# Attention and expert layer on one core: where a planning step and the fifth batch's row scatters stand in the GpSimd queue

## The chip, the cores and the metric

The kernel runs on one core of a Trainium2 chip. The metric is the device time in microseconds (us) of one execution; the time of a kernel is the median of its runs. Engine names are those of the profile: PE (TensorE matmul), PEld (its weight loads), DVE (VectorE), ACT (ScalarE), POOL (GpSimd) and SP (SyncE, which here only issues DMAs). Lines are written L743 for line 743 of the kernel.

## The reference

Attention with rotary embedding over 8 batches, 8 heads, 576 tokens and a head size of 64 gives 4608 rows of 512 numbers; each row then goes to the one of 8 experts that its gate picks.

```python
q_rot, k_rot = rotate(q), rotate(k)
scores = scale * q_rot @ k_rot.T;  attn = softmax(scores)
x = (attn @ v).transpose(0, 2, 1, 3).reshape(N, D)
logits = x @ w_gate + modality_bias[modality_id]
e_idx = argmax(logits, axis=1); gate_w = softmax(logits)[e_idx]
for e in range(E):
    mask = e_idx == e
    out[mask] = gate_w[mask, None] * (relu(x[mask] @ w1[e]) @ w2[e])
```

## The kernel before, in words

**Attention.** The work goes by 32 pairs of heads (numbered 0 to 31, four to a batch). For each pair SP loads the two rotation inputs (`load`, L352); POOL rotates them with four instructions on 128x1152 tiles: the cosine product (`T2`, L466), the sine product (`T1`, L468), their sum (`R`, L470) and, after ACT has written the rounded part `HI` (L457), the rest `LO` (L474). SP then copies both parts into the other half of the partitions (`swap`, L482, keys `SWH` and `SWL`, two DMAs each). PE forms the scores of the pair (`scores`, L497, units S0 to S8) from the parts and their swapped copies, DVE takes minima (L506), ACT exponentials (L515), PE transposes (L520), DVE and ACT copy those out of PSUM (L553, L457), PE multiplies with v (L578) and projects (L613), and DVE scales the output rows (L628 to L632).

**Routing.** After the fourth pair of a batch SP writes its rows to DRAM (`xout`, L638 and L640), and fifteen small steps (RK0 to RK14) on POOL, DVE, ACT and PE find each row's expert and place. Then each of five blocks of rows is loaded back (`back`, keys BK0 to BK4, L761 and L763; on SP for the first five batches, on POOL for the last three) into one of two buffers XL, used in turn, and scattered to its place by a DMA that POOL issues (`scatter`, keys SC0 to SC4, L743). A scatter waits for its block's load; a load waits until the scatter that last used its buffer has landed.

**Planning.** After five batches `plan0` (L785 on) finds which expert's weights the first five blocks of the expert layer need. It is a generator that is run in nine pieces with due times `pl`; a piece is a row of tiny POOL instructions, or one sum on DVE (`total`, L788). The fifth piece is the DVE sum `total(tk, t88)`, whose input the fourth piece writes on POOL (L810 to L817). The ninth is L852 to L863.

**Expert layer.** `m_plan` reads the plan into SP registers, `m_ix` (L1012) loads the row table of a block, which must have been scattered before, `m_rows` (L1035) loads the rows, `m_load1` (L1039) and `m_load2` (L1044) the weights, and PE multiplies (L1089 to L1427).

**The order of the work.** Everything up to the expert layer is a list of jobs with due times: a job of pair n stands at 14.438 n plus its key, from `KEYS` or, for some pairs, from `EDGE`; jobs of the expert layer stand at 14.438 x 31 plus their entry in `MOE`. The list is sorted, and the jobs are written out in that order. PE, ACT, DVE, POOL and SP each keep that order, so on each engine a waiting instruction holds up all that follow it. Due times only order the work; they are not times of the profile.

The jobs that the change concerns stand in this order now. POOL, batches 1 to 4 (n is the batch's last pair): T1 of pair n+10, LO of n+9, T2 of n+10, SC3, R of n+10, RK11, SC4, T1 of n+11, LO of n+10. For the fifth batch (n = 19) SC1 stands behind R of pair 27, SC3 behind LO of 28, SC2 behind T2 of 30, SC4 behind R of 31; its BK2 and BK4 stand in SP's queue among the work of pairs 27 and 28. DVE has the fifth plan piece behind a row minimum (MN8) of pair 25 and ahead of a copy (B_F1) and three more minima of that pair.

Of the kernel before, what the change touches and what calls it, by code (L numbers as in the profile page):

```python
# [25 lines left out]
NSB = 4  # L26
NA = 1 + NSA
NB_MAX = 20
# [27 lines left out]
}  # L56
SLOTS = {
    "S0": 1, "S1": 2, "S2": 3, "S3": 0, "S4": 2, "S5": 0, "S6": 2, "S7": 0, "S8": 1, "F0": 1, "F1": 3, "F2": 0, "F3": 3, "FA": 2,
# [72 lines left out]
        "LD1": -42.214,  # L131
    },
    19: {
        "BK0": 71.4, "BK1": 71.5, "BK3": 95.0, "BK2": 116.0, "BK4": 131.0,
        "SC3": 113.825, "SC2": 128.215, "SC4": 152.075,
    },
# [73 lines left out]
    setdma=(-399.9101, -371.7589, -36.5660, -104.6596),  # L210
    consts=(-3.3332, 30.1765),
    plan=(-34.727, -25.884, -5.857, 16.183),
    ix=(-13.525, 11.679, 11.775, 17.3),
    w1=(-33.501, -27.735, 15.231, -22.655),
    w2=(-4.011, 1.762, 12.647, -8.483),
    hi=(-22.046, 1.027, 19.87, 16.903),
# [8 lines left out]
    l1d=(22.8091, 22.8691, 24.6621, 24.6471),  # L225
    w1n=(20.502, 24.643, 23.254, 22.825),
    place=(14.247, 18.005),
    rows=(-13.5, 11.7, 20.6, 31.756, 31.757),
    pl=(-114.356, -102.856, -99.906, -88.406, -85.506, -73.956, -51.417, -48.907, -45.303),
    end=24.98,  # L230
)
PIN = "PE,Activation,DVE,Pool"
# [3 lines left out]
def tile_attention_moe(ctx: ExitStack, tc: tile.TileContext, qk, v, mod, wg, mb, w1, w2, rope, cf, ci, out):  # L236
# [19 lines left out]
    PLA = cst.tile([1, 3, NA], I32, name="PLA")  # L256
    PLB = cst.tile([1, 3, NSB + NB_MAX + 1], I32, name="PLB")
# [6 lines left out]
    def cview(name):  # L264
        o, n = CF_OFF[name]
        return CF[:, o:o + n]
# [121 lines left out]
    def setup():  # L388
        g = nc.gpsimd
        v_ = nc.vector  # L390
        v_.memset(EPS, 1e-9)
        v_.memset(ZERO, 0.0)
        for t in PD:
            v_.memset(t, 0.0)
        v_.memset(P4, 0.0)
        for t in Vs:
            v_.memset(t[64:128, 0, 4, :], 0.0)
            v_.memset(t[0:64, 1, 4, :], 0.0)
        v_.memset(G, 0.0)
        for t in HL + SW:  # L400
            for c in (0, TW - 64):
                v_.memset(t[:, :, c:c + 64].bitcast(F32), 0.0)
        for h in range(4):
            for s in range(2):
                g.tensor_copy(RW[s * 64:s * 64 + 64, h, :].rearrange("p (o c) -> p o c", o=2)[:, :, 0:32],
                              idf[s * 64:s * 64 + 64, s * 64:s * 64 + 64].rearrange("p (o c) -> p o c", o=2))
        g.memset(MI, 0)
        nonlocal TI
        TI = XG[0].rearrange("p t g f -> p (t g f)")[:, 0:XU]
        g.memset(TI, 0.0)  # L410
        for x in XL:
            g.memset(x[:, XU:XW], 0.0)
        g.memset(TI[:, DM:DM + 1].bitcast(I32), EMPTY)
        g.memset(ON, 1.0)
        g.memset(OH, 0.0)
        g.dma_start(out=CF, in_=cf)
        g.dma_start(out=VAL, in_=ci)
# [363 lines left out]
    def plan0():  # L781
        G_ = nc.gpsimd

        def t1(name, sh):
            return sm.tile([1] + sh, F32, name=name, tag=name, bufs=1)  # L785

        def total(o, i):
            nc.vector.tensor_reduce(o, i, op=ALU.add, axis=AX.X)  # L788

        most = NPL * S // SUP  # L790
        AB = AB9[:, 0:E]
        sl = cview("SL")[0:1]
        EBv = cview("EB")[0:1]
        tri = cview("TRI")[0:1].rearrange("p (a b) -> p a b", b=E)
        nf, nb, cum, ge, tk, a2, rem, hc = (t1(x, [E]) for x in ("nf", "nb", "cum", "ge", "tk", "a2", "rem", "hc"))
        G_.tensor_tensor(nf, RUN[0:1, NPL, :], EBv, op=ALU.subtract)
        th = t1("th", [most])
        G_.tensor_scalar(th, sl[:, 0:most], float(SUP), float(SUP), op0=ALU.mult, op1=ALU.add)
        full = t1("full", [E, most])
        sh = [1, E, most]  # L800
        G_.tensor_tensor(full, nf.unsqueeze(2).to_broadcast(sh), th.unsqueeze(1).to_broadcast(sh), op=ALU.subtract)
        G_.tensor_scalar(full, full, 0.0, None, op0=ALU.is_ge)
        yield
        total(nb, full)
        yield
        t88 = t1("t88", [E, E])
        G_.tensor_tensor(t88, tri, nb.unsqueeze(1).to_broadcast([1, E, E]), op=ALU.mult)
        total(cum, t88)
        yield
        G_.tensor_tensor(tk, cum, nb, op=ALU.subtract)  # L810
        G_.tensor_scalar(tk, tk, float(NSA), None, op0=ALU.min)
        G_.tensor_scalar(a2, cum, float(NSA), None, op0=ALU.min)
        G_.tensor_tensor(a2, a2, tk, op=ALU.subtract)
        G_.tensor_scalar(hc, a2, float(SUP), None, op0=ALU.mult)
        G_.tensor_tensor(rem, nf, hc, op=ALU.subtract)
        G_.tensor_scalar(rem, rem, float(BLK), None, op0=ALU.is_ge)
        G_.tensor_tensor(t88, tri, rem.unsqueeze(1).to_broadcast([1, E, E]), op=ALU.mult)  # L817
        yield
        total(tk, t88)
        yield  # L820
        G_.tensor_scalar(tk, tk, 1.0, None, op0=ALU.is_equal)
        G_.tensor_tensor(rem, rem, tk, op=ALU.mult)
        G_.tensor_scalar(AB, a2, 2.0, None, op0=ALU.mult)
        G_.tensor_tensor(AB, AB, rem, op=ALU.add)
        sh = [1, NSA + 1, E]
        cmp = t1("cmp", [NSA + 1, E])
        cs = cmp[:, 1:NSA + 1, :]
        shs = [1, NSA, E]
        G_.tensor_tensor(cs, cum.unsqueeze(1).to_broadcast(shs), sl[:, 0:NSA].unsqueeze(2).to_broadcast(shs), op=ALU.subtract)
        G_.tensor_scalar(cs, cs, 0.0, None, op0=ALU.is_le)  # L830
        G_.tensor_tensor(cmp[:, 0, :], rem, cview("W8")[0:1], op=ALU.mult)
        yield
        es = t1("pes", [NB_MAX + 1])[:, 0:NA]
        total(es, cmp)
        yield
        G_.tensor_scalar(es[:, 0:1], es[:, 0:1], -1.0, float(E), op0=ALU.mult, op1=ALU.add)
        G_.tensor_scalar(es, es, float(E - 1), None, op0=ALU.min)
        G_.tensor_copy(PLA[:, 0, 0:NA], es)
        ch = t1("ch", [NB_MAX])[:, 0:NSA]
        G_.tensor_tensor(ch, es[:, 1:NA], es[:, 0:NSA], op=ALU.subtract)  # L840
        G_.tensor_scalar(ch, ch, 0.0, None, op0=ALU.is_equal)
        G_.tensor_scalar(PLA[:, 2, 1:NA], ch, -1.0, 1.0, op0=ALU.mult, op1=ALU.add)
        G_.memset(PLA[:, 2, 0:1], 1)
        G_.tensor_scalar(ge, nb, -float(SUP), float(RS), op0=ALU.mult, op1=ALU.add)
        G_.tensor_tensor(cs, cs, ge.unsqueeze(1).to_broadcast(shs), op=ALU.mult)
        G_.tensor_tensor(hc, hc, EBv, op=ALU.add)
        G_.tensor_scalar(hc, hc, float(-E * RS), None, op0=ALU.add)
        G_.tensor_tensor(cmp[:, 0, :], hc, rem, op=ALU.mult)
        yield
        rb = t1("rb", [NB_MAX])[:, 0:NA]  # L850
        total(rb, cmp)
        G_.tensor_scalar(rb[:, 0:1], rb[:, 0:1], float(E * RS), None, op0=ALU.add)  # L852
        r2 = t1("r2", [NB_MAX])[:, 0:NSA]
        G_.tensor_scalar(r2, sl[:, 0:NSA], float(SUP), None, op0=ALU.mult)
        G_.tensor_tensor(rb[:, 1:NA], rb[:, 1:NA], r2, op=ALU.add)
        G_.tensor_scalar(PLA[:, 1, 0:NA], rb, float(E * RS), None, op0=ALU.min)
        e2 = t1("e2", [NSB + 1])
        G_.tensor_scalar(e2[:, 0:1], es[:, NA - 1:NA], 1.0, None, op0=ALU.add)
        G_.memset(PLB[:, 2, NSB + NB_MAX:NSB + NB_MAX + 1], 1)
        G_.memset(CP9[:, 0:1], 0.0)  # L860
        G_.memset(AB9[:, E:E + 1], 0.0)
        G_.tensor_scalar(EB9, sl[:, 0:E + 1], float(RS), None, op0=ALU.mult)
        G_.tensor_scalar(EBN, EBv, float(-E * RS), None, op0=ALU.add)  # L863
        planned_[0] = e2
        yield
# [614 lines left out]

    K = KEYS
    setup()
    pinned = {getattr(mybir.EngineType, x) for x in PIN.split(",")}
    order = ExitStack()
# [62 lines left out]
    def Z(nm, i, f, *a):  # L1547
        J(MOE[nm][i], "moe", z, f, *a)
# [10 lines left out]
    for i in range(2):  # L1559
# [3 lines left out]
        Z("te", i, m_tre, 0, i, 0)  # L1563
        Z("ted", i, m_tre, 0, i, 1)
    g = plan0()
    for i in range(9):
        Z("pl", i, next, g, None)
    end = MOE["end"]
    for i, (s, j) in enumerate(((0, 0), (1, 0), (1, 1), (2, 0), (2, 1))):
# [186 lines left out]
```

## Time and profile before

| what | us |
|---|---|
| median of three runs | 871.61 (868.73 to 873.98) |
| the profiled execution | 869.71 |
| its span, first to last instruction | 867.9 |
| PE busy | 833.6 |
| POOL busy | 460.3 |
| DVE busy | 709.0 |
| ACT busy | 611.8 |

The profile tells of one execution; times in its rows count from the first instruction. An engine's row says when an instruction began, how long it took, its line and what it writes and reads, and in brackets how long the engine stood idle before it and what ended that. SPq rows are the issuing of DMAs, not the transfers. Attention runs until about 460 us, the expert layer from there.

### The profile page before, as it was taken

How to read it: one execution, taken by the hardware profiler on the slowest of the kernel's cores; microseconds unless marked ns; L12 is line 12 of the kernel's file. 1: busy time of each engine (PE TensorE's matmuls, PEld its weight loads, DVE VectorE, ACT ScalarE, POOL GpSimd, SP SyncE). 2: the span in 40 equal slices, each digit the busy share in tenths (PEclk: the TensorE clock that was granted, in tenths of full speed). 3: DMA queues.
4: the chain of work that ended last, by engine and by line, in shares of the span. 5: the costliest groups of instructions: out<-in, count | busy, mean ns of one | idle time of the engine just before them, and what ended most of it. 6: DMA issues, size and time to landing. Idle time of an engine off the chain costs nothing.

```text
span 867.9 us, 24887 instructions
## 1 busy us (share of the span) xinstructions
PE 833.6 (96%) x9528; PEld 689.5 (79%) x9528; DVE 709.0 (82%) x1595; ACT 611.8 (70%) x1311; POOL 460.3 (53%) x372
## 2 busy tenths in 40 slices
PE   2999999999999999899999999999999999999996
PEld 2777777777777777676778989898989898989895
DVE  7788898888888888797898677989898989897562
ACT  2898889898898988796985536565656575656453
POOL 3999979989999899899513123023302020202021
PEclk9999999999999999999999999999999999999999
DMA  8776858969789696875867983357964512531340
GB/s 289 211 242 180 272 158 261 265 203 266 217 257 272 201 276 192 259 223 173 233 197 195 332 227 107 61 179 227 298 173 153 139 50 49 172 97 49 121 142 22
DMA packets 115499, 165.81 MB, mean 191 GB/s; under 512 B 30636, under 2 KB 76350, under 8 KB 115372
## 3 DMA queue, kind: packets, MB, share of 16 engines
q1 hardware_dynamic: 106204, 137.99, 55.4%
q0 software_dynamic: 7824, 24.53, 8.2%
q8 instruction: 77, 1.26, 0.6%
q10 hardware_dynamic: 1344, 1.62, 0.6%
q14 instruction: 50, 0.41, 0.2%
HBM read 118.14 MB, written 34.70 MB: 176 GB/s over the span
## 4 chain that ended last, share of the span: by engine, by line
PE 46%; DVE 2%; POOL 1%; ACT 1%; issue 1%; SPq 1%; DMA 1%; POOLq 0%; ACTq 0%; DVEq 0%
PE psY L1331 20%; PE psH L1207 14%; PE ps L578 2%; PE psY L1207 2%; PE ps L520 1%; PE ps L497 1%; PE psH L1089 1%; PE psY L1108 1%; DMA ST<-in_moe_w_dram 1%; PE ps L1089 1%; PE psH L1403 1%; PE psY L1427 1%; DVE W2L L454 1%; SPq L1035 0%; PE ps L613 0%
## 5 line engine op out<-in xcount | busy, mean ns | idle before, releaser
L506 DVE CUSTOM_DVE_ANT_1 sc<-ps,ZERO 128x576 f32<-128x576 f32 x288 | 206.9, 749 | 23.5 <-PE ps L497 10.1
L515 ACT ACTIVATE P<-sc,mn 128x576 f32<-128x576 f32 x256 | 195.6, 768 | 5.6 <-DVE mn L506 5.0
L497 PE MATMUL ps<-HL 64*128 64x288 f32 x960 | 170.2, 312 | 12.5 <-ACT HL L457 11.3
L497 PE MATMUL ps<-SW 64*128 64x288 f32 x960 | 169.9, 312 | 4.2 <-DVE ST L468 3.6
L497 PEld LDWEIGHTS ps<-HL 64*128 64x128 f32 x960 | 136.3, 190 | 17.7 <-ACT HL L457 11.3
L1119 POOL DMA_INDIRECT out_dram<-sc,ix x36 | 43.8, 1218 | 200.2 <-ACT sc L1118 192.9
L497 PEld LDWEIGHTS ps<-SW 64*128 64x128 f32 x960 | 136.2, 190 | 8.8 <-DVE ST L468 3.9
L578 PE MATMUL ps<-PH,AT 128*64 128x320 f32 (+1 forms) x1024 | 138.2, 412 | 3.8 <-DVE PH L553 3.6
L1207 PE MATMUL psH<-HL,W1H 128*128 128x256 f32 x600 | 126.4, 279 | 0.2 <-ACT HL L457 0.2
L1207 PE MATMUL psH<-HL,W1L 128*128 128x256 f32 x400 | 111.6, 279 | 0.0
L578 PEld LDWEIGHTS ps<-PH,AT 128*64 128x64 f32 x1024 | 67.9, 136 | 52.0 <-DVE PH L553 7.0
L553 DVE COPY PH<-ps 128x512 f32<-128x512 f32 (+1 forms) x160 | 98.4, 631 | 10.0 <-PE ps L520 8.2
L457 ACT ACTIVATE PH<-ps 128x512 f32<-128x512 f32 (+1 forms) x160 | 85.1, 550 | 28.3 <-PE ps L520 23.2
L520 PEld LDWEIGHTS ps<-idf,P 64*128 64x128 f32 x2304 | 86.1, 138 | 21.9 <-ACT P L515 11.5
L1331 PE MATMUL psY<-W2L,SW 128*128 128x512 f32 x256 | 101.3, 396 | 0.0
L520 PE MATMUL ps<-idf,P 64*128 64x64 f32 x2304 | 97.6, 225 | 3.6 <-ACT AT L457 1.4
L1331 PE MATMUL psY<-W2H,SW 128*128 128x512 f32 x256 | 100.9, 394 | 0.0
L1207 PEld LDWEIGHTS psH<-HL,W1H 128*128 128x128 f32 x600 | 98.8, 188 | 1.0 <-ACT HL L457 0.4
L474 POOL TENSOR_TENSOR HL<-ST,HL 128x1152 fp32r<-128x1152 f32 x31 | 82.3, 2656 | 24.9 <-ACT HL L457 24.9
L743 POOL DMA_INDIRECT XS<-XL,oi x40 | 46.1, 1153 | 80.5 <-DMA XL<-X 60.6
L470 POOL TENSOR_TENSOR ST<-ST 128x1152 f32<-128x1152 f32 x30 | 79.7, 2656 | 1.2
L1207 PEld LDWEIGHTS psH<-HL,W1L 128*128 128x128 f32 x400 | 75.2, 188 | 0.0
(286 smaller groups left out, 1835.5 us busy)
## 6 DMA issues: line engine op xcount, KB each, us to landing
ST<-in_moe_w_dram SPq DMA_DIRECT2D x88, 512.0 KB
ST<-in_qk_dram SPq DMA_DIRECT2D x62, 576.0 KB
SW<-HL SPq DMA_DIRECT2D x124, 216.0 KB
AT<-in_v_dram SPq DMA_DIRECT2D x32, 256.0 KB
X<-X SPq DMA_DIRECT2D x8, 1024.0 KB
XL<-X SPq DMA_DIRECT2D x20, 257.0 KB
XG<-XS SPq DMA_DIRECT2D x40, 128.0 KB
XS<-ZR SPq DMA_DIRECT2D x8, 514.0 KB
```

The source lines that it names most:

```text
L457: return nc.scalar.activation(o, i, AF.Copy, scale=scale)
L470: e.tensor_tensor(a, a, b, op=ALU.add)
L474: e.tensor_tensor(d["HL"][:, 1, o], a, d["HL"][:, 0, o].bitcast(F32), op=ALU.subtract)
L497: nc.tensor.matmul(ps[:, g, 0:288], t[:, wq, q0:q0 + P], t[:, wk, k0:k0 + 288], start=(m == 0), stop=(m == len(L) - 1))
L506: nc.vector.tensor_tensor_reduce(sc, d.pop(("S", u))[:, :, 0:288], ZERO.unsqueeze(2).to_broadcast([P, 2, 288]), 1.0, FMAX, ALU.add, ALU.mi ...
L515: nc.scalar.activation(p, sc.rearrange("p a b -> p (a b)"), AF.Exp, bias=mn, scale=-1.0, accum_out=d["sum"][:, u:u + 1])
L520: nc.tensor.transpose(ps[:, g, c:c + 64], src[r, k0:k0 + P], idf[r, r])
L553: alone(d["at", f], g, (nc.vector.tensor_copy if g else acopy)(o, i).ins, int(f[1] in "23B"))
L578: i = nc.tensor.matmul(pa[hh * 64:hh * 64 + 64, 0:c1 - c0], d["V"][:, hh, kt, :], r, start=(kt == 0), stop=(kt == 4))
L743: inst = nc.gpsimd.indirect_dma_start(out=XS, out_offset=bass.IndirectOffsetOnAxis(ap=oi[0:n, j:j + 1], axis=0), in_=xl[b, j][0:n], in_off ...
L1207: nc.tensor.matmul(ps[b][:, r * BLK:r * BLK + BLK], w[:, c, f0:f0 + P], x[:, c, :], start=(first and r == 0 and c == 0 and i == 0), stop=( ...
L1331: nc.tensor.matmul(po[t], hx[:, c, o:o + P], w[:, c, :], start=(k == 0 and c == 2 * q and i == 0), stop=(k == 3 and c == 2 * q + 1 and i = ...
```

## The change

It gives some jobs other due times, cuts the ninth plan piece in two, and moves one memset to the start.

```diff
 KEYS:
-    "SC2": 105.27, "SC3": 118.91, "SC4": 121.32,
+    "SC2": 105.27, "SC3": 109.7, "SC4": 124.1,
 EDGE[19]:
-        "BK0": 71.4, "BK1": 71.5, "BK3": 95.0, "BK2": 116.0, "BK4": 131.0,
-        "SC3": 113.825, "SC2": 128.215, "SC4": 152.075,
+        "BK0": 71.4, "BK1": 71.5, "BK3": 95.0, "BK2": 156.0, "BK4": 156.1, "SC1": 151.5,
+        "SC3": 152.5, "SC2": 159.0, "SC4": 160.0,
 MOE:
-    ix=(-13.525, 11.679, 11.775, 17.3),
+    ix=(-7.2, 11.679, 11.775, 17.3),
-    rows=(-13.5, 11.7, 20.6, 31.756, 31.757),
-    pl=(-114.356, -102.856, -99.906, -88.406, -85.506, -73.956, -51.417, -48.907, -45.303),
+    rows=(-7.0, 11.7, 20.6, 31.756, 31.757),
+    pl=(-114.356, -102.856, -99.906, -88.406, -82.0, -73.956, -51.417, -48.907, -45.303, -15.1),
 setup():
         g.memset(ON, 1.0)
+        g.memset(PLA[:, 2, 0:1], 1)
 plan0():
-        G_.memset(PLA[:, 2, 0:1], 1)
...
         G_.tensor_scalar(PLA[:, 1, 0:NA], rb, float(E * RS), None, op0=ALU.min)
+        G_.memset(PLB[:, 2, NSB + NB_MAX:NSB + NB_MAX + 1], 1)
+        yield
         e2 = t1("e2", [NSB + 1])
         G_.tensor_scalar(e2[:, 0:1], es[:, NA - 1:NA], 1.0, None, op0=ALU.add)
-        G_.memset(PLB[:, 2, NSB + NB_MAX:NSB + NB_MAX + 1], 1)
...
-    for i in range(9):
+    for i in range(10):
         Z("pl", i, next, g, None)
```

In the sorted list this gives the following orders. POOL, batches 1 to 4: T1 of pair n+10, SC3, LO of n+9, T2 and R of n+10, RK11, T1 of n+11, SC4, LO of n+10. Fifth batch on POOL: R of pair 31, SC1, SC3, RK0 of the seventh batch, the new tenth plan piece, SC2, LO of 31, SC4. On SP: ... `xout` of the seventh batch, the v load of pair 30, BK2, BK4, SWL and SWH of 31, the v load of 31, one weight load, then the first block's row table and rows (`ix`, `rows`), which before the change stood right behind SWH of 31. On DVE the fifth plan piece stands behind the copy B_F1 and three minima of pair 25.

## Rows read from the trace of the kernel before

**Rows 1.** The page: busy time of each engine, and the group of the row minima.

```profile
PE 833.6 (96%) x9528; PEld 689.5 (79%) x9528; DVE 709.0 (82%) x1595; ACT 611.8 (70%) x1311; POOL 460.3 (53%) x372
...
L506 DVE CUSTOM_DVE_ANT_1 sc<-ps,ZERO 128x576 f32<-128x576 f32 x288 | 206.9, 749 | 23.5 <-PE ps L497 10.1
```

**Rows 2.** Windows of 20 us: PE, PEld, DVE, ACT, POOL busy, granted clock, DMA share, GB/s.

```profile
340.00:360.00 20.00, 20.00 (x358) 15.52 (x353) 17.95 (x57) 17.45 (x45) 17.82 (x11) 1.00 0.69 203
360.00:380.00 20.00, 17.18 (x260) 12.94 (x260) 16.54 (x51) 16.65 (x43) 18.81 (x25) 1.00 0.88 253
380.00:400.00 20.00, 19.14 (x312) 14.76 (x310) 15.46 (x46) 16.64 (x43) 18.14 (x26) 1.00 0.54 166
400.00:420.00 20.00, 18.61 (x316) 13.97 (x312) 16.20 (x50) 15.97 (x45) 19.27 (x16) 1.00 0.65 186
420.00:440.00 20.00, 20.00 (x317) 15.35 (x319) 16.70 (x46) 18.47 (x48) 6.50 (x9) 1.00 0.86 252
```

**Rows 3.** Timeline of all engines, the plan's fourth and fifth piece.

```profile
362.78 0.31 POOL L817 TENSOR_TENSOR t<-CF,rem 1x64 f32<-1x64 f32 x1
...
363.12 0.21 DVE L788 TENSOR_REDUCE tk<-t 1x8 f32<-1x64 f32 x1 [2.75 <-POOL t L817]
...
363.26 0.67 DVE L553 COPY PH<-ps 128x512 f32<-128x512 f32 x1
...
363.99 2.38 PE L578 MATMUL ps<-PH,AT 128*64 128x320 f32 x16 [2.78 <-DVE PH L553]
```

**Rows 4.** Timeline of POOL, pairs 28 to 31.

```profile
386.80 1.05 POOL L743 DMA_INDIRECT XS<-XL,oi  x1 [0.16 <-issue]
...
404.37 1.09 POOL L743 DMA_INDIRECT XS<-XL,oi  x1 [0.18 <-issue]
...
408.25 2.64 POOL L470 TENSOR_TENSOR ST<-ST 128x1152 f32<-128x1152 f32 x1
...
425.70 2.67 POOL L474 TENSOR_TENSOR HL<-ST,HL 128x1152 fp32r<-128x1152 f32 x1 [2.95 <-ACT HL L457]
```

**Rows 5.** Timeline of POOL, the part of the ninth piece that moves, first and last.

```profile
400.65 0.21 POOL L858 TENSOR_SCALAR e<-pes 1x1 f32<-1x1 f32 x1
...
401.35 0.23 POOL L863 TENSOR_SCALAR EBN<-CF 1x8 f32<-1x8 f32 x1
```

**Rows 6.** Timeline of ACT, pair 30.

```profile
410.93 1.16 ACT L457 ACTIVATE HL<-ST 128x1152 fp32r<-128x1152 f32 x1 [3.31 <-POOL ST L470]
```

**Rows 7.** Timeline of PE, pair 30.

```profile
412.47 1.21 PE L520 MATMUL ps<-idf,P 64*128 64x64 f32 x32 [1.39 <-ACT AT L457]
```

**Rows 8.** Timeline of SP, the queue ahead of pair 31's swaps.

```profile
428.94 1.16 SPq L361 DMA_DIRECT2D AT<-in_v_dram  x2
430.19 2.47 SPq L482 DMA_DIRECT2D SW<-HL  x4
432.93 0.71 SPq L1012 DMA_DIRECT2D ix<-XS  x1
```

**Rows 9.** Timeline of PE, first scores of pair 31.

```profile
437.26 0.38 PE L497 MATMUL ps<-SW 64*128 64x288 f32 x1
```

**Rows 10.** Timeline of SP and of POOL, fifth batch: first block's load and its scatter.

```profile
345.49 0.81 SPq L761 DMA_DIRECT2D XL<-X  x2
...
349.02 1.02 POOL L743 DMA_INDIRECT XS<-XL,oi  x1 [2.18 <-DMA XL<-X]
```

**Rows 11.** Timeline of POOL, sixth batch: a block's load and its scatter.

```profile
468.51 0.59 POOL L761 DMA_DIRECT2D XL<-X  x1 [3.52 <-DMA XS<-XL,oi]
475.89 1.00 POOL L743 DMA_INDIRECT XS<-XL,oi  x1 [6.79 <-DMA XL<-X]
```

**Rows 12.** Timeline of SP and of PE, pair 29: its swaps and first scores.

```profile
399.52 2.79 SPq L482 DMA_DIRECT2D SW<-HL  x4
...
406.07 0.40 PE L497 MATMUL ps<-SW 64*128 64x288 f32 x1
```

**Rows 13.** Windows of 4 us near the start, columns as in rows 2.

```profile
24.00:28.00 4.00, 2.51 (x56) 2.28 (x58) 3.78 (x8) 3.67 (x9) 3.92 (x3) 0.97 1.05 270
28.00:32.00 4.00, 4.00 (x49) 4.00 (x48) 2.53 (x10) 3.73 (x9) 2.12 (x3) 0.60 0.38 109
```

**Rows 14.** Timelines of SP and PE: swaps and first scores around pair 12, then pair 23.

```profile
166.16 1.10 SPq L482 DMA_DIRECT2D SW<-HL  x2
...
175.68 0.29 PE L497 MATMUL ps<-SW 64*128 64x288 f32 x1
...
315.91 1.15 SPq L482 DMA_DIRECT2D SW<-HL  x2
...
325.02 0.40 PE L497 MATMUL ps<-SW 64*128 64x288 f32 x1 [0.42 <-DMA SW<-HL]
```

## The prediction

> **What bounds the kernel now.** I read the page first: PE is busy 833.6 us of the span of 867.9, the next engine 709.0 [rows 1]. So an edit is worth what it takes from, or adds to, the 34 us in which PE is not busy. The windows of 20 us then show where those lie in the stretch that the change touches: PE is busy all of 340 to 360 and of 420 to 440, and short by 2.82, 0.86 and 1.39 us in the three windows between, 5.07 in all [rows 2]. POOL is busy 17.8 to 19.3 us of each 20 from 340 to 420 and only 6.5 in the next one [rows 2]: through these pairs it works without a pause, so whatever stands in its queue delays the rotations behind it; after 420 it has time.
>
> Two gaps make up most of the loss. The first is a chain of three waits: DVE sits 2.75 us in front of the plan's fifth piece until POOL has written its input, the PSUM copy behind it on DVE starts late, and PE waits 2.78 us for that copy [rows 3]. The second is POOL's lateness: R of pair 30 ends at 410.89 [rows 4], ACT, which stood idle 3.31 us for it [rows 6], writes HI, and PE waits 1.39 us for the ACT copy queued behind HI [rows 7].
>
> **The fifth piece on DVE.** Its own 0.21 us stays; it goes behind the copy and three minima. DVE was free at 363.12 - 2.75 = 360.37; the copy takes 0.67 and each minimum 0.75 [rows 1, 3], so it comes to the sum at 363.3, and the input is there at 362.78 + 0.31 = 363.09 [rows 3]. The wait goes, and with it PE's 2.78. Nothing else on DVE asks for the sum, and POOL reads it pairs later. Bounds: 0 to -2.78; I take **-2.78**.
>
> **POOL's queue up to R of pair 30.** SC1, SC3 and SC2 of the fifth batch leave it, each about 1.05 to 1.09 us with 0.17 in front [rows 4], 3.7 together, and so does the end of the ninth plan piece, from 400.65 to 401.58 [rows 5], 0.93. With no idle time to swallow it, R of pair 30 ends 4.6 us earlier, at 406.3. PE, itself 2.78 earlier, would see no wait if R ended by 410.89 - 1.39 - 2.78 = 406.7. So the 1.39 goes too. One thing goes the other way: by pair 29 POOL has lost only two scatters, 2.5 us, while PE is 2.78 ahead, so some 0.3 comes back there. The pairs before that have less again: 27 and 28 are rotated 1.2 us earlier but needed 2.78 earlier, which takes 1.6 of their margin; I count that at nothing, with 1.6 as its bound. **-1.39 + 0.3**, between 0 and -1.39. BK2 and BK4 leave SP's queue there as well, two issues that no wait of PE hangs on.
>
> **The scatters' new place.** SC1 and SC3 come behind R of pair 31, where POOL idles 2.95 us [rows 4] and is 4.6 us ahead besides; they, and the 0.9 us of the tenth piece, cost nothing. SC2 is another matter. It waits for BK2, and SP issues BK2 only behind the v load of pair 30, whose issue ends at 430.10 [rows 8]. That load and the writing of the seventh batch ahead of it wait for buffers that PE and DVE free, so they keep PE's pace: against PE's work BK2 can't go earlier. Behind SC2 on POOL stands LO of pair 31, behind LO on SP its swaps, and behind the swaps on PE the first scores of pair 31, at 437.26 [rows 9]. In PE's time, BK2 is issued where the swaps are issued now, 430.19 [rows 8], 7.1 us ahead of those scores. The new chain:
> - the load, from issue to the start of its scatter: 349.02 - 345.49 = 3.5 us [rows 10] on SP, 475.89 - 468.51 = 7.4 us [rows 11] on POOL amid the weight loads. I take 3.5: same queue, same batch, same sizes;
> - the scatter: 1.1 [rows 4];
> - LO: 2.7 [rows 4];
> - both swaps, from first issue to the scores: their issue alone takes 2.5 [rows 8], and pair 29 had them 406.07 - 399.52 = 6.55 us after the first issue without a wait on PE [rows 12]. I take 4.3, near the middle.
>
> Together 11.6, less 7.1: PE waits **+4.5** us. From the low ends it is 2.3, from the high ends 10.7. BK4 lands beside this chain, and SC4 stands behind LO.
>
> **Row table and rows of the first block.** `ix`, issued at 432.93 now [rows 8], must wait for SC4 to land, so it and the rows go some 10 us later, past a weight load that they no longer hold up; the two weight loads and the plan read behind them go later in turn. PE's expert layer starts near 460, itself shifted by the wait above, which covers them: 0. If the cover were gone, each us late would be one of PE.
>
> **The fourth and fifth scatters of batches 1 to 4.** SC3 now runs ahead of LO of pair n+9, so that LO and its swaps come 1.2 us later. In pair 12 the swaps of LO are issued at 166.16 and first used at 175.68: 9.5 us, which become 8.3. In pair 23, behind the writing of a batch's rows, 325.02 - 315.91 = 9.1 us were not quite enough and PE waited 0.42 [rows 14]. So the cost is between 0 and 0.8 a batch, 3.2 in all; I take 0, since no batch is written just ahead of pair 12's swaps. SC4 passes T1 of pair n+11 only; what stands ahead of LO of n+10 stays the same sum. The two memsets are too short to matter.
>
> **Sum.** 869.71 - 2.78 - 1.39 + 0.3 + 4.5 = 870.3 against the profiled execution. That one lies 1.9 under the median of the three runs, so for a median I say **872.2**: the gain is real and is given back at pair 31.
>
> **The clock.** Near the start PE was busy only 2.51 of 4 us, and in the next window the granted clock fell to 0.60 of full speed, part of it at 1.2 GHz: 0.40 x 4 = 1.6 us lost [rows 13]. The wait of 2.78 us left the clock at 1.00 [rows 2]. A wait of 4.5 lies beyond that. The Trainium skill, page "TensorE: Matmul & The Clock Gate", section "HAM oscillation — how this bites in real kernels", holds that a PE left waiting for data long enough falls back to half clock and has to earn the full one again. By that rule the new wait would cost the 1.6 on top; one row here agrees with it and the other doesn't contradict it.
>
> **Rivals.**
> - *The gain stands.* If BK2's data and the swaps come so fast that the chain is within about a microsecond of 7.1, or POOL's order lets LO go first, PE keeps 3.9: 865.8, as a median 867.7. For it: pair 31's swaps have 7.1 us now and POOL idles. Against it: issue, scatter, LO and swap issue alone make 9.8 with the shortest load seen.
> - *The clock falls in the new wait*: 870.3 + 1.6 = 871.9, as a median 873.8.
> - *Slower: the load is slow.* BK2 queues behind 1 MB of written rows, v and weights. At the 7.4 of rows 11 PE waits 8.4 us at pair 31's first scores, and the clock falls: 870.3 + 3.9 + 1.6 = 875.8, as a median 877.7. It decides from a load of about 6 us on.
> - *The first four batches pay* 0.8 each at pairs 12, 16, 20 and 24: 873.5, as a median 875.4. For it: pair 23 shows how thin the margin can be. Against it: pair 12 itself shows no wait.
>
> **Chances.** Forecast 0.40, on its own 870 to 874.5 (a wait of 2.3 to 6.8 us at pair 31); the gain stands 0.25; the clock 0.15; slow load 0.12; first batches 0.08. What the runs can tell from no change is 0.5%, 4.4 us: faster is below 867.3, slower above 876.0. The gain that stands lies at that edge, so about half of it counts as faster, with little else: 0.14. Slower takes most of the slow load, and a third of the first batches and of a fallen clock that comes with a longer wait: 0.17. The rest is 0.69. The range runs from 866.8, nearly a microsecond under the gain that stands, to 877.3, which leaves out the half of the slow load that is slower still.
>
> **What the profile after would show.** If the steps hold: no DVE wait in front of L788 and no PE gap near 361; ACT's wait for R of pair 30 about 1 us and no PE gap near 411; the row of SC2 with an idle time ended by XL<-X, LO of pair 31 right behind it, and in front of PE's first L497 of pair 31 a wait of 2 to 7 us for SW<-HL. The forecast is wrong if that last wait is missing, if waits for SW<-HL appear in pairs 12 to 24 or 27 to 28, or if the first products of the expert layer wait for their rows.

## The result and the profile after

The changed kernel takes 875.27 us in the median of 22 runs (869.98 to 879.33); the kernel before, run beside it, 868.95 (22 runs). The ratio is 1.0070, 95% interval 1.0055 to 1.0085: it is slower by 0.7%, 6.3 us between the medians, just beyond the 0.5% that was set as the bound of "no change". The profiled execution took 874.81 us, its span is 873.0 at a mean granted clock of 0.994 (867.9 and 0.996 before). Behind line 415 the lines of the changed kernel are one further on: L506 is now L507, L743 is L744.

The windows that answer to [rows 2], with the next 20 us (PE, PEld, DVE, ACT, POOL busy, granted clock, DMA share, GB/s):

```profile
360.00:380.00 20.00, 19.72 (x300) 14.64 (x298) 17.21 (x53) 18.94 (x49) 19.13 (x25) 1.00 0.89 261
380.00:400.00 20.00, 19.80 (x316) 15.19 (x313) 17.08 (x53) 17.25 (x46) 18.09 (x23) 1.00 0.50 131
400.00:420.00 20.00, 20.00 (x338) 15.08 (x336) 17.12 (x50) 18.18 (x45) 17.83 (x14) 1.00 0.71 214
420.00:440.00 20.00, 12.72 (x171) 9.77 (x169) 9.99 (x28) 11.68 (x34) 5.84 (x8) 0.90 0.67 201
440.00:460.00 20.00, 20.00 (x369) 15.98 (x367) 17.48 (x49) 15.36 (x41) 2.53 (x7) 0.93 0.61 174
```

The 5.07 us that PE lacked between 360 and 420 have become 0.48. The price stands in the next window: 7.28 us, and a granted clock of 0.90 and 0.93 where it was 1.00. The gain is what the prediction said. In the timelines of DVE and ACT the plan's fifth piece, now behind the copies and three minima, waits for nothing (2.75 before, [rows 3]), and ACT's wait for R of pair 30 is 1.15 us instead of 3.31 [rows 6]:

```profile
361.43 0.20 DVE L789 TENSOR_REDUCE tk<-t 1x8 f32<-1x64 f32 x1
...
404.32 1.16 ACT L458 ACTIVATE HL<-ST 128x1152 fp32r<-128x1152 f32 x1 [1.15 <-POOL ST L471]
```

The chain of waits from 420 to 440 names every step of the loss (start, duration, what):

```profile
423.73 0.55 SPq L361
...
424.37 4.20 DMA XL<-X
...
429.34 1.04 POOL XS L744
430.39 0.03 issue
430.42 2.63 POOL HL L475
...
433.06 0.50 SPq L483
...
434.29 4.12 DMA SW<-HL
438.41 0.14 issue
438.55 1.50 PE ps L498 x8
```

SP issues the v load of pair 30 (L361) and then BK2 at 424.37; POOL, free since 418.68, starts SC2 when that load has landed, at 429.34; LO of pair 31 stands behind it, the swaps behind LO, and PE behind the swaps. The row of the first scores reads:

```profile
438.55 0.58 PE L498 MATMUL ps<-SW 64*128 64x288 f32 x1 [7.28 <-DMA SW<-HL]
```

Compared matmul by matmul, the 5.1 us by which the span grew come in five pieces. The row of pair 23's first scores stands at 323.56 instead of 325.02 [rows 14]: 1.46 us early. Of these, 0.84 arise between 24 and 33 us, where the kernel before ran in part at 1.2 GHz [rows 13] and this execution of the changed one did not:

```profile
28.00:32.00 4.00, 3.94 (x55) 3.23 (x55) 3.26 (x10) 3.93 (x12) 2.42 (x3) 1.00 0.42 120
```

That drop near 28 us comes and goes: seven of the fourteen profiles have it, a second one of the changed kernel (e5) among them. So this part of the lead is not the change's. Pair 31's scores could have begun at 438.55 - 7.28 = 431.27 instead of 437.26 [rows 9]: another 4.53 us early, the change's gain. The wait makes that 1.29 late. The next rows, of PE in the expert layer, stand at 498.81 against 495.61 before, 3.20 late: 1.9 us more, the clock, for all of it arises while the scores and transposes from 438.55 on run slowly (at 442.78 the changed kernel is already 3.23 late). The last, the rank products at 549.61 against 544.47, are 5.14 late: another 1.9, of which 1.47 is a longer wait (2.58 for 1.11).

```profile
498.81 0.39 PE L1208 MATMUL psH<-SW,W1H 128*128 128x256 f32 x1 [0.34 <-DVE SW L455]
...
549.61 0.18 PE L707 MATMUL psY<-OH,UT 128*128 128x48 bf16 x1 [2.58 <-DVE OH L695]
```

So -1.5 - 4.5 + 7.3 + 1.9 + 1.9 = 5.1. Most of the first is an accident of the two executions; which of the other four belong to the change was the question for the runs.

### The profile page after: what moved, and what is told of

It is laid out like the page before. It is cut to its first block, busy times and chain, and to the rows that moved or that the text cites. A ratio compares the mean times of both kernels' runs of the same rounds, so it can differ in the third digit from the quotient of the medians.

```text
span 873.0 us, 24884 instructions
## 1 busy us (share of the span) xinstructions
PE 834.8 (96%) x9528; PEld 690.2 (79%) x9528; DVE 708.7 (81%) x1595; ACT 612.0 (70%) x1311; POOL 460.6 (53%) x372
## 3 DMA queue, kind: packets, MB, share of 16 engines
q10 hardware_dynamic: 1344, 1.62, 0.6%
## 4 chain that ended last, share of the span: by engine, by line
PE 73%; DMA 9%; POOL 6%; ACT 4%; DVE 3%; issue 2%; SPq 2%; ACTq 0%; POOLq 0%; DVEq 0%
PE psY L1332 21%; PE psH L1208 14%; PE ps L579 12%; PE ps L498 12%; PE ps L521 7%; DMA SW<-HL 3%; PE psY L1208 2%; PE ps L614 2%; DMA ST<-in_moe_w_dram 2%; POOL HL L475 2%; POOL ST L471 2%; DMA XL<-X 1%; PE psH L1090 1%; PE psY L1109 1%; ACT P L516 1%
## 5 line engine op out<-in xcount | busy, mean ns | idle before, releaser
L507 DVE CUSTOM_DVE_ANT_1 sc<-ps,ZERO 128x576 f32<-128x576 f32 x288 | 206.9, 749 | 31.2 <-PE ps L498 17.9
L744 POOL DMA_INDIRECT XS<-XL,oi x40 | 46.4, 1161 | 91.3 <-DMA XL<-X 69.1
```

What stands on the lines that cost most here:

```text
L507: nc.vector.tensor_tensor_reduce(sc, d.pop(("S", u))[:, :, 0:288], ZERO.unsqueeze(2).to_broadcast([P, 2, 288]), 1.0, FMAX, ALU.add, ALU.mi ...
L744: inst = nc.gpsimd.indirect_dma_start(out=XS, out_offset=bass.IndirectOffsetOnAxis(ap=oi[0:n, j:j + 1], axis=0), in_=xl[b, j][0:n], in_off ...
```

## The experiments

Each run has 6 to 12 executions, beside 17 to 35 of the kernel before on the same chip. The medians of before differ from chip to chip (870.1 to 872.2 us), so kernels are compared by the ratio to their own before. The ratios and intervals are those on record; a ratio is not quite the quotient of the two medians (the widest gap is e2's, 0.9969 for 871.65 / 872.16 = 0.9994), so a difference of 0.2% between two ratios says little.

| run | edit | median us | ratio | interval |
|---|---|---|---|---|
| e1 | changed; SC2 behind LO of pair 31 | 871.06 | 0.9982 | 0.9957 to 1.0007 |
| e2 | changed; BK2 ahead of the seventh batch's rows | 871.65 | 0.9969 | 0.9943 to 0.9995 |
| e3, e11 | before; plan's pieces alone | 869.87, 868.95 | 0.9959, 0.9975 | 0.9936 to 0.9982, 0.9954 to 0.9995 |
| e4 | before; SC3, SC4 of batches 1 to 4 alone | 872.76 | 1.0001 | 0.9976 to 1.0026 |
| e5 | changed, again | 876.23 | 1.0056 | 1.0024 to 1.0088 |
| e6 | e1 with batches 1 to 4 as before | 869.49 | 0.9988 | 0.9960 to 1.0015 |
| e7 | changed; plan's pieces as before | 879.97 | 1.0095 | 1.0062 to 1.0128 |
| e8 | changed; BK2 ahead of the v load | 874.82 | 1.0039 | 1.0012 to 1.0066 |
| e9 | e6; SC1 ahead of R of pair 31 | 867.69 | 0.9951 | 0.9928 to 0.9975 |
| e10 | e6; SC1 and SC3 ahead of R of pair 31 | 869.49 | 0.9986 | 0.9965 to 1.0007 |
| e12 | changed; SC1 ahead of R; BK2, BK4 behind the swaps; SC2 behind LO | 870.50 | 1.0010 | 0.9989 to 1.0031 |

The first four tell the parts of the change apart.

**e1: SC2 behind LO.**

```
-        "SC3": 152.5, "SC2": 159.0, "SC4": 160.0,
+        "SC3": 152.5, "SC2": 159.25, "SC4": 160.0,
```

> The third scatter of the fifth batch goes behind LO of pair 31 instead of in front of it; all else is the changed kernel. Theory (the chain load, scatter, LO, swaps makes the wait at pair 31, and the wait brings the half clock): no wait over 1 us on PE in front of pair 31's first scores, no half clock near 436, the gain of about 4.6 us up to pair 31 stays: 868.95 - 4.6 = 864.4 us, between 863 and 866. Rival (the row table and the rows of the first block come too late by then): the wait at pair 31 goes too, but PE waits in the expert layer between 455 and 550 for 3 us or more, and the time is 867 to 869. Rival (the swaps themselves are slow behind the written rows of the seventh batch): a wait of 2 to 4 us for SW stays at pair 31, 867 to 870.

The wait at pair 31 is gone, and so is the half clock there; the ratio falls from 1.0070 (1.0056 in e5) to 0.9982, with intervals well apart. But 864.4 us was not reached, and neither rival shows: no wait for SW at pair 31, none over 1 us in the expert layer before the rank products. The timelines of DVE, PE and POOL show a cost that nobody had on the list:

```profile
421.19 0.76 DVE L507 CUSTOM_DVE_ANT_1 sc<-ps,ZERO 128x576 f32<-128x576 f32 x1 [1.58 <-PE ps L498]
...
422.01 2.37 PE L579 MATMUL ps<-PH,AT 128*64 128x320 f32 x16 [1.63 <-DVE mn L507]
...
418.31 1.10 POOL L744 DMA_INDIRECT XS<-XL,oi  x1 [0.16 <-issue]
419.71 0.99 POOL L744 DMA_INDIRECT XS<-XL,oi  x1 [0.30 <-issue]
```

DVE stands in front of the first row minimum of pair 30 till 421.19. The view names PE's scores, but PE's last score matmul of that stretch started at 420.08, and in the profile of the changed kernel this minimum started 0.85 us behind the first score matmul, here 2.71. SC1 and SC3, side by side, run on POOL in just that time. e6, e9 and e10 take this up.

**e2: the load earlier, SC2 left in front of LO.**

```
-        "BK0": 71.4, "BK1": 71.5, "BK3": 95.0, "BK2": 156.0, ...
+        "BK0": 71.4, "BK1": 71.5, "BK3": 95.0, "BK2": 151.6, ...
```

> The load BK2 goes ahead of the writing of the seventh batch in SP's queue, some 7 us earlier; SC2 stays in front of LO of pair 31. Theory (it is the late load, not the scatter's place on POOL): POOL has its input before it would want it, LO of pair 31 ends by 428, no wait over 1 us at pair 31, no half clock near 436, 864 to 866 us. Rival (the scatter in front of LO is the trouble whatever the load does): a wait of 3 us or more for SW stays at pair 31 and the time stays above 869. Either way BK2 has to wait on SP until the second scatter has read its buffer; if that holds SP for over 2 us, the v load of pair 30 comes later and a new wait for AT would show at pair 30.

Between the two. BK2 did not come 7 us earlier: the timelines of SP, POOL and PE show

```profile
420.63 0.36 SPq L1040 DMA_DIRECT2D ST<-in_moe_w_dram  x1
426.17 0.34 SPq L762 DMA_DIRECT2D XL<-X  x1
426.61 0.61 SPq L639 DMA_DIRECT2D X<-X  x1
...
429.53 1.04 POOL L744 DMA_INDIRECT XS<-XL,oi  x1 [6.55 <-DMA XL<-X]
...
438.93 0.37 PE L498 MATMUL ps<-SW 64*128 64x288 f32 x1 [2.15 <-DMA SW<-HL]
```

SP stands from 421.0 to 426.2 until SC1, which left POOL at 420.44, has read the buffer, 5.7 us. That is the second half of the trap: with two buffers a load can't go earlier than its scatter's landing. The wait at pair 31 is 2.15 us, with a clock of 0.85 from 440 to 450. The wait for AT at pair 30 that was thought of did not come. And the load itself was quick: ahead of the seventh batch's rows, not behind them, it took 429.53 - 426.17 = 3.36 us to the start of its scatter.

**e3 and e11: the plan's pieces alone.** The changed kernel with the fifth batch, the row table, the rows and batches 1 to 4 put back.

> Only the plan's pieces are moved and split; the fifth batch's loads and scatters, the fourth and fifth scatters of batches 1 to 4 and the first block's row table and rows stay where they were before. Theory (two gaps with two causes): the gap of 2.78 us near 361 goes, but POOL is only 0.93 us ahead, so PE, 2.78 us early, waits for R of pair 30 near 411 for 1.39 + 2.78 - 0.93 = 3.2 us; net 2.78 - 1.85 = 0.9 us faster than before, about 868.0 us (867 to 869). Rival (POOL's work follows PE's pace, so both gaps go with the plan piece alone): 868.95 - 4.2 = 864.8 us and no gap over 0.5 us near 411.

> The kernel with the plan's pieces alone moved and split, once more, as the yardstick for the two runs beside it. Theory (two gaps with two causes): no wait near 361, waits of 2 to 3.5 us in all for R or HI of pairs 28 to 30 between 370 and 415, no stall of DVE over 0.5 us in front of pair 30's first row minima (one scatter runs there, not two); ratio 0.996, within 0.998 and 0.9935. Rival (its ratio of 0.9959 owed much to clock that by chance did not fall): 0.998 to 1.000.

The gap at 361 is gone and others take its place, as the first theory said, but spread. In e3 PE waits

```profile
372.95 0.53 PE L521 MATMUL ps<-idf,AT 64*128 64x64 f32 x10 [0.62 <-DVE mn L507]
...
374.51 1.34 PE L521 MATMUL ps<-idf,P 64*128 64x64 f32 x32 [0.91 <-DVE mn L507]
...
389.37 0.26 PE L521 MATMUL ps<-idf,P 64*128 64x64 f32 x1 [0.45 <-issue]
...
399.13 0.71 PE L521 MATMUL ps<-idf,P 64*128 64x64 f32 x16 [0.72 <-ACT P L516]
...
412.70 1.46 PE L521 MATMUL ps<-idf,P 64*128 64x64 f32 x40 [0.66 <-ACT AT L458]
```

3.36 us in all, 3.50 in e11, against 2.14 in that stretch before (0.28, 0.47 and 1.39). Compared matmul by matmul with before, e3's PE gains 2.85 us near 361 and has 1.2 of them left at 413; e11's gains 2.86 and has 1.0 left. That is close to the 0.9 of the first theory. The times are further under before than that: 3.6 and 2.2 us by the ratio, 2.3 and 2.1 by the medians. The clock makes part of it: its mean over e3's runs was 0.9966 against 0.9946 for before, which is 0.0020 x 870 = 1.7 us.

**e4: batches 1 to 4 alone.**

```
-    "SC2": 105.27, "SC3": 118.91, "SC4": 121.32,
+    "SC2": 105.27, "SC3": 109.7, "SC4": 124.1,
```

> Only the fourth and fifth scatters of batches 1 to 4 are moved, on the kernel before. Theory: nothing waits for them, 869.0 us, within 1 us of before, and the gaps of PE up to pair 27 are those of before. Rival (each batch pays where LO is 1.2 us later): new waits for SW<-HL of 0.4 to 0.8 us in pairs 12, 16, 20 and 24, 870.5 to 872 us.

The ratio is 1.0001, and PE's waits over 0.15 us between 150 and 355 us are 0.24, 0.45 and 0.82 against 0.47, 0.40, 0.42 and 0.33 before, 1.51 in all for 1.62: no cost, as forecast. The kind of wait is another, though. All three of e4's are for SW (at pairs 11, 15 and 23); of before's only the 0.42 at pair 23 is, and the others are for copies of DVE. Over that stretch the waits for SW add up to 0.42 to 2.30 us in the eight profiles with the new places and to 0 to 1.11 in the six with the old, those of all kinds to 0.60 to 3.12 and 1.33 to 2.22. They stand at pairs 11, 15, 19 and 23 for the most part, and none at pairs 12, 16, 20 and 24, where the rival has them. The run tells something else. Its wait near 361 is that of before (3.02 us to 2.78), yet the window from 360 to 370 has a granted clock of 0.83 (e4 first, then the kernel before):

```profile
360.00:370.00 10.00, 6.98 (x69) 4.08 (x66) 4.71 (x14) 5.02 (x14) 9.22 (x13) 0.83 0.94 273
```

```profile
360.00:370.00 10.00, 7.22 (x118) 5.32 (x116) 6.65 (x19) 7.13 (x18) 9.22 (x14) 1.00 0.95 283
```

**e5, e7, e8: what sets the wait.** e5 is the changed kernel again. e7 takes back the plan's pieces, their times and the cut in two:

```
-    pl=(-114.356, -102.856, -99.906, -88.406, -82.0, -73.956, -51.417, -48.907, -45.303, -15.1),
+    pl=(-114.356, -102.856, -99.906, -88.406, -85.506, -73.956, -51.417, -48.907, -45.303),
```

e8 puts BK2 in front of pair 30's v load ("BK2": 152.1 for 156.0).

> The changed kernel itself once more, beside the next three on one chip, for what recurs in its profile. Theory (a chain of fixed steps makes the wait at pair 31): the wait in front of pair 31's first scores is there again, 6.5 to 8 us long, half clock follows it, and the time is 0.7% over before. Rival (the 7.28 us were one slow load): the wait is 4 to 5.5 us in this profile and the ratio falls to 1.003. The wait for OH near 547, 2.58 us in the first profile of this kernel and 1.11 before, is not tied to the change in either; if it recurs at 2.5 it is.

> The fifth batch's loads and scatters, the first block's row table and rows, and the places in batches 1 to 4 as changed, but the plan's pieces in their places of before. Theory (the chain at pair 31 keeps PE's pace, so what the plan's fifth piece saves is not swallowed by the wait): PE waits 2.8 us near 361 as before, not near 411, and 6.5 to 8 us at pair 31 with half clock behind; the time is 2 to 3 us over that of the changed kernel. Rival (the chain keeps time of its own, and PE only runs ahead into the wait): the wait at pair 31 is shorter by 2.8 us, about 4.5, and the time is that of the changed kernel within 0.5 us.

> The changed kernel with the load BK2 in front of the v load of pair 30 instead of behind it in SP's queue; SC2 stays in front of LO of pair 31. Theory (each us that BK2 is issued earlier is one less at pair 31): BK2 is issued some 2.5 us earlier against PE's work, the wait at pair 31 is 4.7 us (4 to 5.5), half clock follows for 3.4 or 6.8 us, and the time is 2.5 us or a little more under that of the changed kernel. Rival (the load waits for the second scatter to have read its buffer, which took 5.7 us in the run with the load still further ahead): BK2 is issued no earlier than 5.5 us behind that scatter, 421.8 us if it is issued where it was, so the two agree on the load; but where the scatter lands later still, SP stands, and the wait is 5.5 to 7 us.

The starts of the steps, from the timelines of SP, POOL and PE (us); the last column is from BK2's issue to the scores:

| | BK2 | SC2 | LO | swaps | scores | PE's wait | chain |
|---|---|---|---|---|---|---|---|
| changed | 424.37 | 429.34 | 430.42 | 433.06 | 438.55 | 7.28 | 14.18 |
| e5 | 425.69 | 430.28 | 431.35 | 434.03 | 439.61 | 5.50 | 13.92 |
| e7 | 433.61 | 438.50 | 439.51 | 442.16 | 447.67 | 7.71 | 14.06 |
| e8 | 424.27 | 429.94 | 431.01 | 433.70 | 439.28 | 3.99 | 15.01 |

The chain is 13.9 to 15.0 us in each: fixed steps, not one slow load. e5's wait of 5.50 missed the 6.5 to 8 that were expected and lies at the edge of what the rival gave; its chain of 13.92 and its ratio of 1.0056 speak against the rival. In e7, where PE waits for the plan's piece again (2.13 us), the wait is not shorter but 7.71: BK2 keeps PE's pace, so what PE gains ahead of it is not swallowed. Its time is 0.39% over e5's, 3.4 us, with intervals that overlap a little. In e8 BK2 is issued 435.28 - 424.27 = 11.0 us ahead of where the scores would begin, against 6.9 in the changed kernel, and the wait is 3.99, at the low end of the 4 to 5.5 expected; the ratio is lower than e5's by 0.17%, 1.5 us, with intervals that overlap. e5's wait is shorter because its BK2 has 434.11 - 425.69 = 8.4 us of head start for 6.9. Where the 1.5 come from was not tried; DVE's stall, seen in e1, held PE up 1.23 us near 419, and if SP's queue did not share that, it is most of them.

**e6, e9, e10: the stall.** In the seven profiles with SC1 and SC3 side by side behind R of pair 31 (changed, e1, e2, e5, e6, e7, e8), DVE stood 0.93 to 1.72 us in the first row minima of pair 30 in six, and PE 0.98 to 1.63 behind it in five; in the three without the pair (before, e3, e4), never. The seventh is the first profile of the changed kernel, where SC1 and SC3 ran from 415.04 to 417.43 beside the same minima: the pair alone does not make the stall. e6 repeats e1 with batches 1 to 4 as before; e9 and e10 move the scatters.

```
e9   -  "SC1": 151.5, "SC3": 152.5,
     +  "SC1": 148.9, "SC3": 152.5,
e10  +  "SC1": 148.9, "SC3": 149.0,
```

> The third scatter of the fifth batch behind LO of pair 31 and besides the fourth and fifth scatters of batches 1 to 4 back at their places of before. Theory (those places cost nothing; the stall of 1.6 us in front of pair 30's row minima in the first kernel of this order was one execution's): same time as that kernel within 0.2%, 1.5 to 4 us under before, no wait over 1 us at pair 31 and none near 421. Rival (the stall belongs to this order): DVE stands 1 us or more in front of the same row minima again and PE 1.2 us or more in front of the attention product behind them.

> On the kernel with the third scatter behind LO of pair 31 and batches 1 to 4 as before: the second scatter goes one place up in POOL's queue, in front of R of pair 31, so that the two scatters no longer follow each other beside the first row minima of pair 30. Theory (DVE's stall there, 0.9 to 1.7 us in six of the seven profiles with the two scatters side by side and in none of the three without, comes from the pair of them): no DVE stall over 0.5 us in front of those row minima, no wait of PE over 0.5 us near 419, no wait over 1 us at pair 31, and the time is 1 us under the kernel without this edit, 3 us or more under before (ratio 0.9965 or less). Rival (the stall comes from PE's or DVE's own lead there, the scatters have nothing to do with it): DVE stalls 0.9 us or more at the same row minima again; ratio 0.998 to 1.000.

> As the run beside it, with both the second and the fourth scatter in front of R of pair 31. Theory (the two scatters side by side hold up DVE wherever DVE then is): no stall in front of the first row minima of pair 30, but one of 0.9 to 1.7 us on DVE some 2.7 us earlier in its queue, among the copies and the row minimum of pair 29; whether PE waits for that depends on who needs it. R of pair 31 ends 2.5 us later than it did, and LO of pair 31, which POOL waited 2.9 us to start, hides it. Rival (DVE's stall stays at pair 30's first row minima though no scatter runs there): a wait of PE of about 1 us near 419 as before this edit.

e6 has the stall again, 0.93 us of DVE and 0.98 of PE, just under the 1 and 1.2 that its rival named: it is not one execution's. In e9 it is gone. Timelines of DVE, POOL and PE:

```profile
416.29 0.75 DVE L507 CUSTOM_DVE_ANT_1 sc<-ps,ZERO 128x576 f32<-128x576 f32 x1
...
412.99 1.09 POOL L744 DMA_INDIRECT XS<-XL,oi  x1
414.11 2.66 POOL L471 TENSOR_TENSOR ST<-ST 128x1152 f32<-128x1152 f32 x1
416.93 1.00 POOL L744 DMA_INDIRECT XS<-XL,oi  x1 [0.17 <-issue]
...
432.92 0.37 PE L498 MATMUL ps<-SW 64*128 64x288 f32 x1 [1.08 <-DMA SW<-HL]
```

The minimum starts as the first unit of scores is done, and PE does not wait near 419. By the ratio e9 is 0.49% faster than before, 4.3 us (3.4 between the medians): the gain of the changed kernel without its losses, and faster than both kernels. Whether it is faster than the plan's pieces alone is not shown: e11, beside it on the same chip, has 0.9975, and the intervals overlap. The 1.08 at pair 31 were a miss against "no wait over 1 us". In e10 DVE's stall is gone too; the one foretold 2.7 us earlier did not come (the longest idle of DVE there is 0.76 us). But e10's ratio, 0.9986, is e6's and not e9's, though its profile has neither the stall nor a wait at pair 31; so how much of a kernel's time goes with the stall the ratios do not tell. So two scatters side by side on POOL go with the stall only where they met those minima; by what they hold DVE up, no run shows.

**e12: the loads behind the swaps.**

```
-  "BK2": 156.0, "BK4": 156.1, "SC1": 151.5, "SC3": 152.5, "SC2": 159.0, "SC4": 160.0,
+  "BK2": 159.7, "BK4": 159.75, "SC1": 148.9, "SC3": 152.5, "SC2": 159.9, "SC4": 160.0,
```

> The changed kernel with three moves in its fifth batch: the second scatter in front of R of pair 31; the third and fifth scatter behind LO of pair 31; and their two loads behind the swaps of pair 31 in SP's queue. The places in batches 1 to 4 and all else are the changed kernel's. Theory (what is to be first in each queue is what PE waits for next): no DVE stall at pair 30's first row minima, no wait over 0.3 us at pair 31 where the run with the loads ahead of the swaps had 1.08, and the places in batches 1 to 4 cost nothing: 4.5 to 5.5 us under before, ratio 0.9935 to 0.9955. Rival (the late scatters hold up what follows them): SC2 and SC4 come some 3 us later, and with them the routing of the seventh batch on POOL and the row table; a new wait of PE of 1 us or more between 435 and 500, ratio 0.996 or more.

The rival won. The wait for SW at pair 31 is gone, but SC2 starts at 437.05 where e9 has 430.76, 2.8 us later against PE's work (pair 31's scores, without e9's wait, are 3.5 later), and behind SC2 and SC4 on POOL stands the routing of the seventh batch. Timelines of POOL, DVE and PE:

```profile
437.05 1.05 POOL L744 DMA_INDIRECT XS<-XL,oi  x1 [10.78 <-DMA XL<-X]
...
440.11 0.27 POOL L683 TENSOR_TENSOR vv<-vv,CF 128x40 f32<-128x40 f32 x1
...
440.41 0.20 DVE L686 TENSOR_REDUCE vm<-vv 128x5 f32<-128x40 f32 x1 [2.24 <-POOL vv L683]
...
443.78 0.37 PE L498 MATMUL ps<-SW 64*128 64x288 f32 x1 [1.70 <-DVE PH L554]
```

DVE waits 2.24 us for POOL, the copy behind it is late, PE waits 1.70, and the window from 440 to 450 has a clock of 0.83. The wait and the slow matmuls behind it make 3.3 of the 5.1 us that lie between the ratios of e12 and e9; the rest is not explained. It is the pattern of [rows 3] over again, one queue further on.

## Why the prediction was right or wrong

- **The fifth piece (-2.78) and POOL's queue (-1.39 + 0.3)**: right. Their sum of 3.9 measured 4.53 in the profile, with the small waits of before at 388 and 398 gone as well. e3 and e11 show that the one needs the other: with POOL nearly as full as before, over half of the 2.78 comes back before 415.
- **SC1 and SC3 cost nothing**: wrong, though the first profile hides it. Idle time on POOL was taken as cover; what suffered was DVE. It goes with a wait of PE of about 1 us in five of seven profiles. Between e6 (0.9988) and e9 (0.9951) lie 3.2 us, more than that wait, and e10 (0.9986) has no stall either, so that the stall is what separates the two is not shown.
- **The new wait (+4.5)**: the step that failed, by its size. The mechanism and the place were right, and 7.28 lies inside 2.3 to 10.7 (the low ends add up to 9.8, which less 7.1 is 2.7, not 2.3). Load to scatter took 4.97 for the 3.5 of [rows 10], the first swap to the scores 5.49 for 4.3; scatter and LO were as told (1.08, 2.64), and the head start 6.90 for 7.1. Together 14.18 for 11.6. The 3.5 was taken because it was the same queue and sizes; it had been read where no batch's rows had just been written. e2 agrees, with 3.36 us ahead of the seventh batch's rows; behind them the load took 4.59 to 5.67 in e5, e7 and e8. But behind the swaps, in e12, it took 437.05 - 431.10 = 5.95, so the rows are not all that slows it; which transfers do, no run tells apart.
- **The clock**: put down as a rival of 0.15, where it belonged in the forecast. From the wait on the granted clock is 0.81 and 0.85 in windows of 10 us, part of them at 1.2 GHz, and the 2.4 GHz level is back at 443. It cost 1.9 us, not far from the 1.6 of [rows 13]:

```profile
430.00:440.00 10.00, 2.73 (x23) 1.98 (x21) 1.38 (x4) 2.16 (x7) 5.18 (x8) 0.81 0.59 161
440.00:450.00 10.00, 10.00 (x169) 8.49 (x167) 8.09 (x25) 6.72 (x17) 0.75 (x3) 0.85 0.66 192
```

  The mean granted clock over the runs of e5 is 0.9917 against 0.9958 for before: 0.0041 x 870 = 3.6 of its 4.9 us at most. The Trainium skill, page "TensorE: Matmul & The Clock Gate", section "HAM oscillation — how this bites in real kernels", lays half clock to PE's waits for data; the long waits here agree, and the short ones are told of below.
- **The row table and the rows, and batches 1 to 4 (0 each)**: right. The row table is issued at 439.26 instead of 432.93 [rows 8], and no product of the expert layer waits for it; e4 is at 1.0001. Waits for SW in pairs 12 to 24, named as a sign that the forecast is wrong, did show (0.76 at pair 19 and 0.40 at pair 23 in the changed kernel, 0.42 at pair 23 before), but not at the pairs whose LO comes later, and the waits of all kinds in that stretch came to 1.42 for 1.62: the sign was too wide.
- **Not foreseen**: the longer wait for the rank products near 547. It is 2.58 and 2.57 in the two profiles of the changed kernel and 1.11 before, but 1.86 in e4, which has nothing of the change near it, and 0.67 to 2.43 in the ten others. Whether part of it is the change's stays open.
- **The median**: the forecast moved the sum up by 1.9 because three runs had a median of 871.61; over 22 runs before stood at 868.95. The time held, 875.27 within 866.8 to 877.3, but of the difference only 0.6 of 6.3 us was forecast, and "slower" had 0.17. That the time lies in the range is in part luck: set on 868.95, the same sums would give 869.5 and a range that ends at 874.6.

## What to carry to other kernels

A step moved into an engine's idle time carries its own wait with it: ask what it waits for, what is queued behind it on that engine, and cost the whole chain to the engine that sets the end, with the slower of two loads seen when other traffic is beside it. Put first in each queue what PE waits for next; here one place up for SC1 and one place down for SC2 (with batches 1 to 4 as before, which cost nothing in e4) turned a loss of 0.6% into a gain of 0.5%, and one place too far down cost the gain again. A wait of several us on PE is priced with the clock that falls behind it.

## What the runs showed of the hardware

- The granted clock does not fall by the length of a wait alone. In the fourteen profiles, from 20 us on, half clock followed all four waits of PE of 3.99 to 7.71 us, and 11 of the 32 between 1.0 and 3.1 us: behind 1.16 (e11, near 497) it fell, behind the 2.78 of before it didn't, and behind the same wait in e4 (3.02) it did. (The waits before 20 us are left out: the windows show a clock of 1.00 there, but one score matmul takes 0.44 us, as behind the wait of 7.28, and 0.29 later.) The drop of [rows 13] was not there in the profile of the changed kernel (1.00 from 28 to 32). Much of the spread of one kernel's runs, 8 us and more, may be this; that is argued from the clocks of the runs, not tried.
- In e2 a scatter held its source buffer for 5.7 us after it had left POOL, and the next load of that buffer stood 5.2 us on SP for it.
- Two scatters side by side on POOL, where they met the first row minima of a pair, went with a DVE stall of 0.93 to 1.72 us in six of seven profiles, which the timeline laid to PE in five of them; none of the other seven had it. How it comes about, no run shows.
